# The first batch of a linear-attention and MLP kernel, rescheduled over four engines

## The chip, the cores and the metric

The kernel runs on one NeuronCore of a Trainium2 chip. The metric is the device time of one execution, in microseconds (us). TensorE (PE) does the matrix products, VectorE (DVE) and ScalarE (ACT) work on SBUF and on PSUM, [...] and SyncE (SP) issues most of the DMA transfers.

## The reference

Eight batches of eight heads, 576 positions and 64 features each go through a linear attention with cosine weights. Its output, 4608 tokens by 512, goes through an MLP with a Swish that has a factor for each hidden unit.

```python
def phi(x, c, s):
    r = np.maximum(x, 0.0)
    return np.concatenate([r * c, r * s], axis=-1)
q_p, k_p = phi(q, cos_w, sin_w), phi(k, cos_w, sin_w)   # angle pi/2 * pos / 576
kv = np.einsum('bhsf,bhsd->bhfd', k_p, v)
z = np.sum(k_p, axis=2)
num = np.einsum('bhsf,bhfd->bhsd', q_p, kv)
den = np.einsum('bhsf,bhf->bhs', q_p, z)[..., None] + 1e-06
x = (num / den)  # transposed and reshaped to 4608 x 512
h = x @ w_in     # 512 x 2048
g = h * (1.0 / (1.0 + np.exp(-beta * h)))
out = g @ w_out  # 2048 x 512
```

## The kernel before

**Tiling.** A position is p*9+n, with p from 0 to 63 on the partitions and n, the block, from 0 to 8. Two heads sit in the two halves of the partitions, and four such groups j side by side; jp counts pairs of them. A batch thus has nine blocks (n = 0 to 8) of 64 positions. The MLP takes tokens in chunks of 512, which are eight blocks: chunk 0 is blocks 0 to 7 of batch 0, and chunk 1 begins with block 8 of batch 0, followed by seven blocks of batch 1. There are nine chunks.

**One batch.** `q_relu` casts the queries to `qb` with a ReLU; PE (or, from batch 2 on, a DMA) transposes them to `qt`. `qs` is `qt` times the tangent of the angle (`tanr`), so that the cosine can be left out of numerator and denominator; `eps9` is the small constant over the cosine. `k_relu` casts the keys to `rk`. `v_scale` makes two copies of the values in `vb`, one times the cosine, one times the sine. `kv_mm` is the product of keys and values, `kv_take` its copy to SBUF. `num_mm` makes the numerators and denominators of one block for one jp (eight small matmuls), `x_rden` the reciprocal denominators, `x_mul` (DVE) or `x_mul_act` (ACT) the quotient `xs`. `x_turn_pe` transposes it on PE and copies it to `xt`, the moving operand of the MLP.

**The MLP.** Each chunk takes 32 slots. In slots 0 to 15, `h_group(c, jt)` makes one tile of 128 hidden units (four matmuls of 512 columns) and its Swish (`h_act`). In slots 16 to 31, `o_part` makes a quarter of an output tile; in chunk 0 the quarters go round, so that each block of `wout` is needed as late as can be. The weights are loaded in FP32 into four stage buffers and cast to BF16: `w_in` first, and each `w_out` block into the stage that a cast has freed. SP issues, after the first batch: w_out 0, w_out 1, value and key of batch 1, w_out 2, query of batch 1, w_out 3.

**Order.** Under `manual_schedule` each engine runs its instructions in the order in which the code issues them. The first batch is written out by hand ahead of the loop (lines 432 to 501), with dummy matmuls on zeros (`warm_pe`). Then, still ahead of the loop, the weights' casts and the first work on batch 1 are issued, in this order (lines 502 to 519):

```python
    cast_wout(0)
    cast_wout(1)
    v_scale(1, 0)
    k_relu(1)
    cast_wout(2)
    q_relu(1, 0)
```

Then the loop over the slots of chunk 0 follows. After each slot it issues what the table `early` (line 527) holds for it: block 8's transposes in slot 4, the rest of batch 1 from slot 15 on. Batches 2 to 7 are spread over the slots of the later chunks (`att_units`).

**Load gates.** Two DMAs of four bytes, `gate <- rk`, wait for key casts; on SP they stand ahead of the loads of w_in 1 and of w_in 2 and 3.

**Block 8 before.** Blocks 7 and 8 have their own PSUM banks in the first batch (4 and 6). ACT scales them, and block 8 of jp 1 comes after the xt copy.

Of the kernel before, what the change touches and what calls it, by code (L numbers as in the profile page):

```python
# [10 lines left out]
FP32 = mybir.dt.float32  # L11
BF16 = mybir.dt.bfloat16
AF = mybir.ActivationFunctionType
ALU = mybir.AluOpType
# [8 lines left out]
def kernel(  # L23
# [64 lines left out]
    def load_w(kind, i, step=4):  # L88
        if (kind, i) not in stages:
            stages[kind, i] = stage.tile([P, 4, 512], FP32, name="w_stage", tag="w_stage")  # L90
        st = stages[kind, i]
        if kind == "out":
            nc.sync.dma_start(out=st, in_=w_out_v[:, 4 * i : 4 * i + 4, :])
            return
        for a in range(0, 4, step):
            nc.sync.dma_start(out=st[:, a : a + step], in_=w_in_v[:, a : a + step, i * 512 : (i + 1) * 512])
# [41 lines left out]
    for g in range(2):  # L138
        nc.gpsimd.iota(it9[g * HP : (g + 1) * HP], pattern=[[1, NQ]], base=0, channel_multiplier=NQ,
                       allow_small_or_imprecise_dtypes=True)  # L140
    halfpi = const.tile([P, 1], FP32, name="halfpi")
    nc.vector.memset(halfpi, math.pi / 2.0)
    zero_b = const.tile([P, 1], FP32, name="zero_b")
# [8 lines left out]
    nc.scalar.activation(sin9, it9, AF.Sin, bias=zero_b, scale=ANG)  # L152
    nc.scalar.activation(warm, zero_b, AF.Silu, scale=1.0)

    zeros = const.tile([P, 512], BF16, name="zeros")
    nc.vector.memset(zeros, 0.0)
    ones = const.tile([HP, P], FP32, name="ones")
    nc.vector.memset(ones, 1.0)
    identf = const.tile([HP, HP], FP32, name="identf")
    make_identity(nc, identf)  # L160
    ident = const.tile([P, P], BF16, name="ident")
    make_identity(nc, ident)

    gate = const.tile([1, 2], BF16, name="gate")


    vb = one.tile([P, NQ, 4, 2, E], BF16, name="vb")
# [6 lines left out]

    nc.vector.reciprocal(eps9, cos9)
    nc.vector.tensor_tensor(tan9, eps9, sin9, op=ALU.mult)

    tdiag = const.tile([HP, NQ, HP], FP32, name="tdiag")
    nc.vector.tensor_tensor(
        tdiag, identf.unsqueeze(1).to_broadcast([HP, NQ, HP]),  # L180
        tan9[0:HP].unsqueeze(2).to_broadcast([HP, NQ, HP]), op=ALU.mult)
    nc.vector.tensor_scalar(eps9, eps9, scalar1=EPS, scalar2=None, op0=ALU.mult)
    for cs, t in ((0, cos9), (1, sin9)):
        nc.vector.tensor_copy(vb[:, :, :, cs, D], t.unsqueeze(2).to_broadcast([P, NQ, 4]))
# [15 lines left out]
    def q_relu(b, jp, eng="dve"):  # L200
        relu(qb[:, jp].rearrange("q n (j d) -> q j n d", j=2), raw_tile(b, "q")[:, 2 * jp : 2 * jp + 2], eng)

    def k_relu(b, j0=0, j1=4, eng="dve", n0=0, n1=NQ):
        relu(rk.rearrange("q n j d -> q j n d")[:, j0:j1, n0:n1], raw_tile(b, "k")[:, j0:j1, n0:n1], eng)

    def v_scale(b, cs, jp=None, n0=0, n1=NQ, eng="dve"):
        t = (cos9, sin9)[cs]
        rv = raw_tile(b, "v")
        js = slice(0, 4) if jp is None else slice(2 * jp, 2 * jp + 2)
        if jp is not None and eng != "act":  # L210
            if eng == "dve":
                t = ps[:, 0, 16 * cs : 16 * cs + NQ]
            (nc.gpsimd if eng == "pool" else nc.vector).tensor_tensor(  # L213
                vb[:, n0:n1, js, cs, 0:D],
                rv.rearrange("q j n d -> q n j d")[:, n0:n1, js],
                t[:, n0:n1].unsqueeze(2).unsqueeze(3).to_broadcast([P, n1 - n0, 2, D]), op=ALU.mult)
            return
        for n in range(n0, n1):
            o, a = vb[:, n, js, cs, 0:D], rv[:, js, n, :]
            if eng == "act":  # L220
                nc.scalar.activation(o, a, AF.Copy, scale=t[:, n : n + 1])
            else:
                nc.vector.tensor_scalar(o, a, scalar1=t[:, n : n + 1], scalar2=None, op0=ALU.mult)  # L223
# [6 lines left out]
    def q_turn_pe(b, jp, bank, hold=False):  # L230

        parts = ((0, 0, 5), (1, 5, NQ))
        v2 = []
        for i, n0, n1 in parts:
            t = ps[:, bank + i].bitcast(BF16)[:, 0 : (n1 - n0) * P].rearrange("q (n c) -> q n c", c=P)
            v2.append(t)
            for n in range(n0, n1):
                nc.tensor.matmul(t[:, n - n0, :], lhsT=qb[:, jp, n, :], rhs=ident,  # L238
                                 is_transpose=True, start=(n == n0), stop=(n == n1 - 1))
        def take(e, i):  # L240
            _, n0, n1 = parts[i]
            if e == "act":
                nc.scalar.copy(qt[:, jp, n0:n1], v2[i])
            else:
                tan_mul(nc.vector, qs[:, jp, n0:n1], v2[i], n0, n1)

        if hold:
            return take
        for e, i in (("act", 0), ("dve", 1), ("act", 1), ("dve", 0)):
            take(e, i)  # L250
# [22 lines left out]
    def kv_take(jps, bank, eng="dve"):  # L273
        a0, a1 = jps[0], jps[-1] + 1
        o = kv[:, :, a0:a1].rearrange("q g s c e -> q g (s c e)")
        a = ps[:, bank : bank + 2, a0 * 2 * E : a1 * 2 * E]
        if eng == "act":
            nc.scalar.copy(o, a)  # L278
        else:
            nc.vector.tensor_copy(o, a)  # L280
# [141 lines left out]
    def warm_pe(count, w=512, bank=1):  # L422
        for i in range(count):
            nc.tensor.matmul(ps[:, bank, 0:w], lhsT=zeros[:, 0:P], rhs=zeros[:, 0:w], start=True, stop=True)  # L424
# [1 line left out]
    beta = const.tile([P, JT], FP32, name="beta")  # L426
    rbeta = const.tile([P, JT], FP32, name="rbeta")

    warm_pe(78, 40)
    q_relu(0, 0, "act")  # L430
    for bank, n0, n1 in ((6, 0, 5), (7, 5, NQ)):
        nc.tensor.matmul(ps[:, bank, 0 : (n1 - n0) * HP], lhsT=ones,  # L432
                         rhs=tdiag[:, n0:n1, :], start=True, stop=True)
    for bank, n0, n1 in ((6, 0, 5), (7, 5, NQ)):
        nc.scalar.copy(tanr[:, n0:n1, :].rearrange("q n p -> q (n p)"), ps[:, bank, 0 : (n1 - n0) * HP])
    nc.tensor.transpose(ps[:, 1, 0:JT], beta16, identf[0:JT, 0:JT])
    nc.vector.tensor_copy(ps[:, 0, 0:NQ], cos9)
    nc.vector.tensor_copy(ps[:, 0, 16 : 16 + NQ], sin9)
    nc.vector.tensor_copy(beta, ps[:, 1, 0:JT])
    nc.vector.reciprocal(rbeta, beta)  # L440
    q_relu(0, 1, "dve")
    warm_pe(5, 128)
    q_turn_pe(0, 0, 4)
    warm_pe(4, 128)
    take = q_turn_pe(0, 1, 2, hold=True)
    warm_pe(9)
    take("act", 0)
    v_scale(0, 1, 0, eng="pool")
    v_scale(0, 0, 0)
    k_relu(0, 0, 2, "act")  # L450
    take("dve", 1)
    take("dve", 0)
    take("act", 1)
    kv_mm(0, 0, 6)
    v_scale(0, 1, 1, eng="pool")
    v_scale(0, 0, 1)
    kv_take((0,), 6, eng="act")
    k_relu(0, 2, 3, "act")
    k_relu(0, 3, 4, "dve", 0, 5)
    k_relu(0, 3, 4, "act", 5, NQ)  # L460

    nc.sync.dma_start(out=gate, in_=rk[0:1, 0, 0, 0:2])
    load_w("in", 1)
    nc.sync.dma_start(out=gate, in_=rk[0:1, 0, 3, 0:2])
    load_w("in", 2)
    load_w("in", 3)
    warm_pe(1, bank=1)
    for n in range(7, NQ):
        num_mm(n, 0, 4, n - 7)
    for n in range(7):  # L470
        num_mm(n, 0, 2, n)
    kv_mm(0, 1, 6)
    warm_pe(2, bank=1)
    got2 = x_rden(4, 0, 7, NQ, (0,))
    got = x_rden(2, 0, 0, 7, (0,))
    kv_take((1,), 6, eng="act")
    x_mul(got, 0, 7)
    x_mul_act(got2, 7)
    x_mul_act(got2, 8)
    for n in range(7, NQ):  # L480
        num_mm(n, 1, 6, n - 7)
    for n in range(7):
        num_mm(n, 1, 0, n)
    for gj in GJ:
        cast_win(0, gj, "pool", jps=slice(0, 1))
    for gj in GJ:
        cast_win(0, gj, "pool", 0, 256, slice(1, 2))
    x_turn_pe(0, 0, 8, 2, jps=(0,))
    got2 = x_rden(6, 0, 7, NQ, (1,))
    got = x_rden(0, 0, 0, 7, (1,))  # L490
    x_mul(got, 0, 4)
    x_mul(got, 4, 7)
    x_mul_act(got2, 7)
    h_mm(0, 0, (0, 1))
    x_turn_pe(0, 0, 4, 4, ("dve",), (1,))
    h_mm(0, 1, (0, 1))
    x_turn_pe(0, 4, 8, 5, ("act",), (1,))
    x_mul_act(got2, 8)
    h_mm(0, 2, (0, 1))
    h_mm(0, 3, (0, 1))  # L500
    for gj in GJ:
        cast_win(0, gj, "dve", 256, 512, slice(1, 2))
# [19 lines left out]
    def num_seven(jp, bank):  # L522
        for n in range(7):
# [1 line left out]

    takes = []
    early = {
        4: lambda: x_turn_pe(0, 8, 9, 7),
        15: lambda: v_scale(1, 1, eng="act"),
        22: lambda: (kv_mm(1, 0, 6), kv_mm(1, 1, 6), q_relu(1, 1), kv_take((0, 1), 6)),  # L530
        24: lambda: (cast_wout(3, "aadd"), takes.append(q_turn_pe(1, 0, 4, hold=True))),
        25: lambda: (takes.append(q_turn_pe(1, 1, 6, hold=True)),
                     [takes[jp](e, i) for jp in range(2)
                      for e, i in (("act", 0), ("dve", 1), ("act", 1), ("dve", 0))]),
        28: lambda: (num_seven(0, 4), num_seven(1, 6), x_mul(x_rden(4, 0, 0, 7, (0,)), 0, 7)),
        29: lambda: (x_turn_pe(1, 0, 7, 4, ("act",), (0,)), x_mul(x_rden(6, 0, 0, 7, (1,)), 0, 7)),
        31: lambda: ([h_mm(1, jt, (0, 1)) for jt in range(2)], x_turn_pe(1, 0, 7, 5, ("dve",), (1,)),
                     [h_mm(1, jt, (0, 1)) for jt in range(2, 4)]),
    }
# [88 lines left out]
```

## Time and profile before

| what | value |
| --- | --- |
| time, median of 3 runs | 299.46 us (298.69 to 299.69) |
| profiled execution: its own time | 301.22 us |
| profiled execution: its span | 299.4 us |
| PE busy | 286.8 us, 96% of the span |
| DVE, ACT, POOL busy | 113.8, 141.4, 74.0 us |
| mean granted PE clock | 0.989 |
| DMA over the first 60 us | 20.18 MB, mean 336 GB/s |

The span runs from the first instruction to the last; the execution's own time has 1.8 us around it. All times in the text are from the span's start. "Busy" of PE includes the drain that the profile models, so it isn't PE at its peak; the granted clock is given beside it, 1.00 for full and 0.50 for half. In a line of the timeline, the columns are start, duration, engine, line of the code, operation, out and in, shape and count, and in brackets the idle time before it and what ended that.

### The profile page before, as it was taken

The numbers are of one execution on the slowest core, as the hardware profiler recorded it, in microseconds if no ns is written. First come the engines' busy times: TensorE is split into PE (matmuls) and PEld (weight loads), VectorE is DVE, ScalarE is ACT, GpSimd is POOL, SyncE is SP. The second block draws the span as 40 slices with busy tenths as digits, with TensorE's granted clock in tenths as the row PEclk, the third lists the DMA queues.
The fourth block names the chain that finished last, engine by engine and source line by source line (L and its number), as shares of the span: only waits on it lengthen the run. The fifth ranks groups of instructions, "written<-read, shape, count | busy, mean of one in ns | idle before, by whom it ended". The sixth has DMA issues, their size and how long they took to land.

```text
span 299.4 us, 7162 instructions
## 1 busy us (share of the span) xinstructions
PE 286.8 (96%) x3042; PEld 143.7 (48%) x3068; DVE 113.8 (38%) x282; ACT 141.4 (47%) x224; POOL 74.0 (25%) x88
## 2 busy tenths in 40 slices
PE   7959999999999999999999999999999999999994
PEld 6633455445544554455445544554455444444443
DVE  3869856591860077006800680059004000000000
ACT  6645765475128512860276117611761178128511
POOL 1550000516156014701270147014701210000000
PEclk9987999999999999999999999999999999999999
DMA  7999999769699349943995299419301920131032
GB/s 244 384 341 340 390 388 391 217 138 396 123 187 376 126 63 189 345 182 66 192 315 207 48 196 342 189 39 177 86 2 20 158 48 0 37 70 35 0 72 70
DMA packets 50264, 53.82 MB, mean 180 GB/s; under 512 B 30888, under 2 KB 31160, under 8 KB 50232
## 3 DMA queue, kind: packets, MB, share of 16 engines
q1 hardware_dynamic: 47512, 46.01, 51.7%
q0 software_dynamic: 2688, 7.34, 10.5%
q8 instruction: 24, 0.39, 0.6%
q14 instruction: 8, 0.07, 0.1%
q10 hardware_dynamic: 32, 0.01, 0.0%
HBM read 36.71 MB, written 9.44 MB: 154 GB/s over the span
## 4 chain that ended last, share of the span: by engine, by line
PE 92%; DVE 3%; ACT 2%; issue 1%; DVEq 0%; ACTq 0%
PE ps L374 42%; PE ps L399 40%; PE ps L289 3%; PE ps L268 3%; PE ps L415 1%; DVE qs L226 1%; PE ps L348 1%; DVE vb L213 1%; ACT g_t L381 1%; PE ps L432 1%; PE ps L238 1%; ACT xt L353 1%; ACT L151 0%; DVE xs L311 0%; PE ps L424 0%
## 5 line engine op out<-in xcount | busy, mean ns | idle before, releaser
L374 PE MATMUL ps<-xt,win 128*128 128x512 bf16 x576 | 130.4, 384 | 2.5 <-ACT xt L353 1.1
L399 PE MATMUL ps<-wout,g_t 128*128 128x512 bf16 x536 | 120.4, 379 | 2.3 <-issue 1.5
L381 ACT ACTIVATE g_t<-ps,beta 128x512 bf16<-128x512 f32 x144 | 98.7, 688 | 37.7 <-PE ps L374 37.7
L374 PEld LDWEIGHTS <-win 128*128 128x128 bf16 x576 | 56.2, 99 | 70.4 <-issue 4.3
L399 PEld LDWEIGHTS <-g_t 128*128 128x128 bf16 x560 | 53.9, 98 | 64.3 <-issue 0.5
L394 POOL DMA_DIRECT2D out_dram<-o_sb x56 | 35.3, 634 | 148.7 <-ACT o_sb L405 148.7
L405 ACT COPY o_sb<-ps 128x512 f32<-128x512 f32 x35 | 20.5, 586 | 99.6 <-PE ps L399 99.6
L226 POOL TENSOR_TENSOR qs<-qt,tanr 128x1152 bf16<-128x1152 bf16 x12 | 29.2, 2452 | 9.1 <-DVE vb L223 8.4
L280 DVE CAST kv<-ps 128x520 bf16<-128x520 f32 x7 | 4.9, 698 | 68.1 <-PE ps L268 68.1
L418 DVE COPY o_sb<-ps 128x256 f32<-128x256 f32 x1 | 0.4, 425 | 63.2 <-PE ps L415 63.2
L311 DVE TENSOR_TENSOR xs<-ps,rden 128x768 bf16<-128x768 f32 (+3 forms) x24 | 22.3, 935 | 1.0 <-DVE rden L304 0.2
L223 DVE TENSOR_SCALAR vb<-raw_v,cos 128x256 bf16<-128x256 f32 x63 | 17.1, 346 | 0.9 <-DMA raw_v<-in_v_dram 0.9
L300 DVE TENSOR_TENSOR den<-ps,eps 128x12 f32<-128x12 f32 (+3 forms) x25 | 4.1, 162 | 33.5 <-PE ps L289 33.4
L223 DVE TENSOR_SCALAR vb<-raw_v,sin 128x256 bf16<-128x256 f32 x54 | 14.7, 346 | 0.0
L289 PEld LDWEIGHTS <-qt 64*64 64x64 bf16 x576 | 10.5, 105 | 4.2 <-issue 4.2
L289 PE MATMUL ps<-kv,qt 64*64 64x65 bf16 x576 | 11.6, 195 | 0.2 <-ACT kv L278 0.2
L289 PE MATMUL ps<-kv,qs 64*64 64x65 bf16 x576 | 11.5, 193 | 0.0
L198 DVE TENSOR_SCALAR qb<-raw_q 128x1152 bf16<-128x1152 f32 x15 | 10.6, 747 | 1.3 <-DMA raw_q<-in_q_dram 1.3
L289 PEld LDWEIGHTS <-qs 64*64 64x64 bf16 x576 | 10.5, 105 | 0.0
L268 PEld LDWEIGHTS <-rk 64*64 64x64 bf16 x576 | 8.6, 106 | 3.9 <-issue 3.3
L268 PE MATMUL ps<-vb,rk 64*64 64x130 bf16 x576 | 10.2, 218 | 0.3 <-DVE vb L213 0.2
L108 DVE CAST win<-w_stage 64x512 bf16<-64x512 f32 (+2 forms) x20 | 10.0, 502 | 0.4
(58 smaller groups left out, 101.9 us busy)
## 6 DMA issues: line engine op xcount, KB each, us to landing
raw_v<-in_v_dram SPq DMA_DIRECT2D x7, 1152.0 KB, 11.4
raw_k<-in_k_dram SPq DMA_DIRECT2D x7, 1152.0 KB, 14.3
raw_q<-in_q_dram SPq DMA_DIRECT2D x7, 1152.0 KB, 7.3
out_dram<-o_sb POOLq DMA_DIRECT2D x56, 128.0 KB, 3.6
w_stage<-in_moe_w_out_dram SPq DMA_DIRECT2D x4, 1024.0 KB, 9.8
w_stage<-in_moe_w_in_dram SPq DMA_DIRECT2D x3, 1024.0 KB, 6.6
out_dram<-o_sb SPq DMA_DIRECT2D x14, 128.0 KB, 2.4
raw_q<-in_q_dram SPq DMA_DIRECT2D x2, 576.0 KB, 3.9
```

Source lines behind the costliest of these rows:

```text
L108: nc.vector.tensor_copy(o, a)
L198: nc.vector.tensor_scalar(dst, src, scalar1=0.0, scalar2=None, op0=ALU.max)
L223: nc.vector.tensor_scalar(o, a, scalar1=t[:, n : n + 1], scalar2=None, op0=ALU.mult)
L226: eng.tensor_tensor(dst.rearrange("q n (g p) -> q n g p", g=2), src.rearrange("q n (g p) -> q n g p", g=2), tanr[:, n0:n1].unsqueeze(2).to ...
L268: nc.tensor.matmul(t[jj * HP : (jj + 1) * HP, g], lhsT=rk[hs, n, 2 * jp + jj, :], rhs=vb[hs, n, 2 * jp + jj].rearrange("q s e -> q (s e)") ...
L289: nc.tensor.matmul(ps[cols, bank + jj, slot * E : (slot + 1) * E], lhsT=(qt, qs)[cs][rows, jp, n, cols], rhs=kv[rows, g, jp, cs, :], start ...
L311: nc.vector.tensor_tensor(o.rearrange("q j n s d -> q j (n s) d"), nv[:, :, a:z, :, 0:D].rearrange("q j n s d -> q j (n s) d"), rden[:, :, ...
L374: nc.tensor.matmul(ps[:, h_bank(c, jt)], lhsT=win[jt // 4][:, mi, (jt % 4) * P : (jt % 4 + 1) * P], rhs=xt[:, :, jp, g * HP : (g + 1) * HP ...
L381: nc.scalar.activation(g_t, ps[:, h_bank(c, jt)], AF.Silu, scale=beta[:, jt : jt + 1])
L394: eng.dma_start(out=out_v[bb, n][:, m0:m1], in_=o_sb[hf * HP : (hf + 1) * HP, m0:m1])
L399: nc.tensor.matmul(o_ps, lhsT=gs[c, jt][:, tt * P : (tt + 1) * P], rhs=wout[jt // 4][:, jt % 4, :], start=(jt == 0), stop=(jt == JT - 1))
L405: nc.scalar.copy(o_sb, o_ps)
```

## The change

The first batch is written anew, and part of it is moved:

- `zeros` is set in two pieces, the first 128 columns first. The first dummies are 58 of 48 columns, not 78 of 40.
- The tangent is spread over the partitions by nine FP32 transposes with a broadcast operand, not by two FP32 matmuls on ones; `tdiag` and `ones` go. DVE copies it to SBUF, not ACT.
- Both query casts are DVE's, ahead of the copies of cosine and sine to PSUM (the second cast after them). The scaled queries take another order.
- The sine copies of the values are split: GpSimd has blocks 0 to 5 (jp 0) and 0 to 4 (jp 1), ACT the rest, one block at a time. The key cast of jp 0 is split between ACT and DVE.
- The key cast of the last group on DVE stands behind the first denominators.
- The two gates go.
- Block 8 leaves the first batch. Its numerators are issued after slot 3, its denominators and quotient after slot 4 (DVE), its transposes after slot 7.
- Block 7 of jp 1 is scaled by DVE; ACT makes both last copies to `xt`; dummies of 512 columns are put in at two more places.
- In chunk 0, batch 1's steps from slot 24 on come one slot later; the cast of w_out 3 comes two later.

```diff
-    warm_pe(78, 40)
-    q_relu(0, 0, "act")
+    warm_pe(58, 48)
     for bank, n0, n1 in ((6, 0, 5), (7, 5, NQ)):
-        nc.tensor.matmul(ps[:, bank, 0 : (n1 - n0) * HP], lhsT=ones,
-                         rhs=tdiag[:, n0:n1, :], start=True, stop=True)
+        for n in range(n0, n1):
+            nc.tensor.matmul(ps[:, bank, (n - n0) * HP : (n - n0 + 1) * HP],
+                             lhsT=tan9[0:HP, n : n + 1].to_broadcast([HP, P]), rhs=identf,
+                             is_transpose=True, start=(n == n0), stop=(n == n1 - 1))
+    nc.tensor.transpose(ps[:, 1, 0:JT], beta16, identf[0:JT, 0:JT])
     for bank, n0, n1 in ((6, 0, 5), (7, 5, NQ)):
-        nc.scalar.copy(tanr[:, n0:n1, :].rearrange("q n p -> q (n p)"), ps[:, bank, 0 : (n1 - n0) * HP])
-    nc.tensor.transpose(ps[:, 1, 0:JT], beta16, identf[0:JT, 0:JT])
+        nc.vector.tensor_copy(tanr[:, n0:n1, :].rearrange("q n p -> q (n p)"), ps[:, bank, 0 : (n1 - n0) * HP])
+    q_relu(0, 0)
+    nc.vector.tensor_copy(beta, ps[:, 1, 0:JT])
     nc.vector.tensor_copy(ps[:, 0, 0:NQ], cos9)
     nc.vector.tensor_copy(ps[:, 0, 16 : 16 + NQ], sin9)
-    nc.vector.tensor_copy(beta, ps[:, 1, 0:JT])
+    q_relu(0, 1)
+    warm_pe(8, 128, bank=0 + 2)
+    q_turn_pe(0, 0, 4)
     nc.vector.reciprocal(rbeta, beta)
-    q_relu(0, 1, "dve")
-    warm_pe(5, 128)
-    q_turn_pe(0, 0, 4)
     warm_pe(4, 128)
     take = q_turn_pe(0, 1, 2, hold=True)
-    warm_pe(9)
+    warm_pe(7)
     take("act", 0)
-    v_scale(0, 1, 0, eng="pool")
+    take("dve", 1)
+    v_scale(0, 1, 0, 0, 6, eng="pool")
+    take("act", 1)
+    v_scale(0, 1, 0, 6, NQ, eng="act")
     v_scale(0, 0, 0)
-    k_relu(0, 0, 2, "act")
-    take("dve", 1)
+    k_relu(0, 0, 2, "act", 0, 5)
+    k_relu(0, 0, 2, "dve", 5, NQ)
     take("dve", 0)
-    take("act", 1)
     kv_mm(0, 0, 6)
-    v_scale(0, 1, 1, eng="pool")
+    v_scale(0, 1, 1, 0, 5, eng="pool")
     v_scale(0, 0, 1)
     kv_take((0,), 6, eng="act")
+    v_scale(0, 1, 1, 5, NQ, eng="act")
     k_relu(0, 2, 3, "act")
-    k_relu(0, 3, 4, "dve", 0, 5)
     k_relu(0, 3, 4, "act", 5, NQ)
-
-    nc.sync.dma_start(out=gate, in_=rk[0:1, 0, 0, 0:2])
-    load_w("in", 1)
-    nc.sync.dma_start(out=gate, in_=rk[0:1, 0, 3, 0:2])
-    load_w("in", 2)
-    load_w("in", 3)
-    warm_pe(1, bank=1)
-    for n in range(7, NQ):
-        num_mm(n, 0, 4, n - 7)
+    for i in range(1, 4):
+        load_w("in", i)
+    warm_pe(1)
     for n in range(7):
         num_mm(n, 0, 2, n)
+    num_mm(7, 0, 4, 0)
+    got = x_rden(2, 0, 0, 7, (0,))
+    got2 = x_rden(4, 0, 7, 8, (0,))
+    k_relu(0, 3, 4, "dve", 0, 5)
+    warm_pe(2, bank=1)
     kv_mm(0, 1, 6)
...
     x_turn_pe(0, 0, 8, 2, jps=(0,))
-    got2 = x_rden(6, 0, 7, NQ, (1,))
     got = x_rden(0, 0, 0, 7, (1,))
+    got3 = x_rden(6, 0, 7, 8, (1,))
     x_mul(got, 0, 4)
     x_mul(got, 4, 7)
-    x_mul_act(got2, 7)
+    x_mul(got3, 7, 8)
+    warm_pe(3, bank=3)
     h_mm(0, 0, (0, 1))
-    x_turn_pe(0, 0, 4, 4, ("dve",), (1,))
     h_mm(0, 1, (0, 1))
+    x_turn_pe(0, 0, 4, 4, ("act",), (1,))
+    h_mm(0, 2, (0, 1))
     x_turn_pe(0, 4, 8, 5, ("act",), (1,))
-    x_mul_act(got2, 8)
-    h_mm(0, 2, (0, 1))
     h_mm(0, 3, (0, 1))
...
     early = {
-        4: lambda: x_turn_pe(0, 8, 9, 7),
+        3: lambda: (num_mm(8, 0, 2, 0), num_mm(8, 1, 2, 1)),
+        4: lambda: x_mul(x_rden(2, 0, 8, NQ, (0, 1)), 8, NQ),
+        7: lambda: x_turn_pe(0, 8, 9, 6),
         15: lambda: v_scale(1, 1, eng="act"),
         22: lambda: (kv_mm(1, 0, 6), kv_mm(1, 1, 6), q_relu(1, 1), kv_take((0, 1), 6)),
-        24: lambda: (cast_wout(3, "aadd"), takes.append(q_turn_pe(1, 0, 4, hold=True))),
-        25: lambda: (takes.append(q_turn_pe(1, 1, 6, hold=True)),
+        25: lambda: (takes.append(q_turn_pe(1, 0, 4, hold=True))),
+        26: lambda: (takes.append(q_turn_pe(1, 1, 6, hold=True)), cast_wout(3, "aadd"),
```

More of the change, by code (lines that the diff above doesn't have):

```diff
@@ L140 @@
                        allow_small_or_imprecise_dtypes=True)
+    zeros = const.tile([P, 512], BF16, name="zeros")
+    nc.vector.memset(zeros[:, 0:P], 0.0)
     halfpi = const.tile([P, 1], FP32, name="halfpi")
@@ L153 @@
     nc.scalar.activation(warm, zero_b, AF.Silu, scale=1.0)
[L155 to L158, printed above, removed]
+    nc.vector.memset(zeros[:, P:512], 0.0)
     identf = const.tile([HP, HP], FP32, name="identf")
@@ L162 @@
     make_identity(nc, ident)
-    gate = const.tile([1, 2], BF16, name="gate")
     vb = one.tile([P, NQ, 4, 2, E], BF16, name="vb")
@@ L176 @@
     nc.vector.tensor_tensor(tan9, eps9, sin9, op=ALU.mult)
[L178 to L181, printed above, removed]
     nc.vector.tensor_scalar(eps9, eps9, scalar1=EPS, scalar2=None, op0=ALU.mult)
@@ L463 @@
-    load_w("in", 1)
-    nc.sync.dma_start(out=gate, in_=rk[0:1, 0, 3, 0:2])
-    load_w("in", 2)
-    load_w("in", 3)
-    warm_pe(1, bank=1)
-    for n in range(7, NQ):
-        num_mm(n, 0, 4, n - 7)
+    for i in range(1, 4):
+        load_w("in", i)
+    warm_pe(1)
     for n in range(7):
         num_mm(n, 0, 2, n)
+    num_mm(7, 0, 4, 0)
[3 more added lines that the diff above has]
+    warm_pe(2, bank=1)
     kv_mm(0, 1, 6)
-    warm_pe(2, bank=1)
@@ L474 @@
-    got2 = x_rden(4, 0, 7, NQ, (0,))
-    got = x_rden(2, 0, 0, 7, (0,))
     kv_take((1,), 6, eng="act")
@@ L478 @@
     x_mul_act(got2, 7)
-    x_mul_act(got2, 8)
-    for n in range(7, NQ):
-        num_mm(n, 1, 6, n - 7)
+    warm_pe(1, bank=1)
     for n in range(7):
         num_mm(n, 1, 0, n)
+    num_mm(7, 1, 6, 0)
     for gj in GJ:
@@ L488 @@
     x_turn_pe(0, 0, 8, 2, jps=(0,))
-    got2 = x_rden(6, 0, 7, NQ, (1,))
     got = x_rden(0, 0, 0, 7, (1,))
+    got3 = x_rden(6, 0, 7, 8, (1,))
     x_mul(got, 0, 4)
     x_mul(got, 4, 7)
-    x_mul_act(got2, 7)
+    x_mul(got3, 7, 8)
+    warm_pe(3, bank=3)
     h_mm(0, 0, (0, 1))
-    x_turn_pe(0, 0, 4, 4, ("dve",), (1,))
     h_mm(0, 1, (0, 1))
+    x_turn_pe(0, 0, 4, 4, ("act",), (1,))
+    h_mm(0, 2, (0, 1))
     x_turn_pe(0, 4, 8, 5, ("act",), (1,))
-    x_mul_act(got2, 8)
-    h_mm(0, 2, (0, 1))
     h_mm(0, 3, (0, 1))
@@ L527 @@
     early = {
-        4: lambda: x_turn_pe(0, 8, 9, 7),
+        3: lambda: (num_mm(8, 0, 2, 0), num_mm(8, 1, 2, 1)),
+        4: lambda: x_mul(x_rden(2, 0, 8, NQ, (0, 1)), 8, NQ),
+        7: lambda: x_turn_pe(0, 8, 9, 6),
         15: lambda: v_scale(1, 1, eng="act"),
         22: lambda: (kv_mm(1, 0, 6), kv_mm(1, 1, 6), q_relu(1, 1), kv_take((0, 1), 6)),
-        24: lambda: (cast_wout(3, "aadd"), takes.append(q_turn_pe(1, 0, 4, hold=True))),
-        25: lambda: (takes.append(q_turn_pe(1, 1, 6, hold=True)),
+        25: lambda: (takes.append(q_turn_pe(1, 0, 4, hold=True))),
+        26: lambda: (takes.append(q_turn_pe(1, 1, 6, hold=True)), cast_wout(3, "aadd"),
                      [takes[jp](e, i) for jp in range(2)
                       for e, i in (("act", 0), ("dve", 1), ("act", 1), ("dve", 0))]),
-        28: lambda: (num_seven(0, 4), num_seven(1, 6), x_mul(x_rden(4, 0, 0, 7, (0,)), 0, 7)),
-        29: lambda: (x_turn_pe(1, 0, 7, 4, ("act",), (0,)), x_mul(x_rden(6, 0, 0, 7, (1,)), 0, 7)),
+        29: lambda: (num_seven(0, 4), num_seven(1, 6), x_mul(x_rden(4, 0, 0, 7, (0,)), 0, 7)),
+        30: lambda: (x_turn_pe(1, 0, 7, 4, ("act",), (0,)), x_mul(x_rden(6, 0, 0, 7, (1,)), 0, 7)),
         31: lambda: ([h_mm(1, jt, (0, 1)) for jt in range(2)], x_turn_pe(1, 0, 7, 5, ("dve",), (1,)),
```

## The prediction

> **What bounds the kernel now.** I read the page first: TensorE (PE) is busy 96% of the span and holds 92% of the chain of waits, so a change counts only where it moves PE. The slices then show where PE is not at full worth: the first three (22 us) are thin, and the granted clock dips there.
>
> ```profile
> PE   7959999999999999999999999999999999999994
> DVE  3869856591860077006800680059004000000000
> PEclk9987999999999999999999999999999999999999
> DMA  7999999769699349943995299419301920131032
> ```
>
> The windows put numbers on the dip: us, then busy time of PE, PEld, DVE, ACT and POOL with counts, clock, DMA share, GB/s.
>
> ```profile
> 17.00:18.20 1.20, 0.10 (x3) 0.03 (x1) 1.17 (x3) 1.10 (x2) 1.10 (x3) 1.00 0.82 172
> 18.20:19.90 1.70, 0.71 (x5) 0.30 (x5) 0.01 (x1) 0.34 (x2) 1.39 (x4) 1.00 0.85 312
> 19.90:22.40 2.50, 1.64 (x8) 0.93 (x9) 1.94 (x7) 0.83 (x3) 0.00 (x0) 0.50 1.05 405
> 22.40:26.70 4.30, 4.27 (x11) 1.48 (x11) 4.12 (x9) 1.53 (x3) 0.00 (x0) 0.50 1.02 360
> 28.30:37.80 9.50, 9.50 (x46) 4.29 (x46) 8.47 (x22) 7.67 (x12) 0.00 (x0) 1.00 1.03 387
> ```
>
> PE works 0.81 of 2.9 us from 17.0 to 19.9, then runs at half clock to 26.7 and without a hole from 28.3. DMA is full throughout. Last, the timeline of DVE and of PE, since block 8 now leaves the first batch and enters DVE's queue elsewhere:
>
> ```profile
> 31.18 3.26 DVE L117 TENSOR_SCALAR wout<-w_stage,rbeta 128x512 bf16<-128x512 f32 x8
> 35.34 2.45 DVE L223 TENSOR_SCALAR vb<-raw_v,cos 128x256 bf16<-128x256 f32 x9 [0.90 <-DMA raw_v<-in_v_dram]
> 38.36 1.36 DVE L198 TENSOR_SCALAR rk<-raw_k 128x2304 bf16<-128x2304 f32 x1 [0.57 <-DMA raw_k<-in_k_dram]
> 41.08 1.67 DVE L117 TENSOR_SCALAR wout<-w_stage,rbeta 128x512 bf16<-128x512 f32 x4 [1.36 <-DMA w_stage<-in_moe_w_out_dram]
> 44.07 1.43 DVE L198 TENSOR_SCALAR qb<-raw_q 128x1152 bf16<-128x1152 f32 x2 [1.31 <-DMA raw_q<-in_q_dram]
> 45.41 0.69 DVE L280 CAST kv<-ps 128x520 bf16<-128x520 f32 x1
> ```
>
> ```profile
> 28.21 0.27 PE L348 MATMUL ps<-ident,xs 128*128 128x128 bf16 x2
> 28.32 9.66 PE L374 MATMUL ps<-xt,win 128*128 128x512 bf16 x44
> 37.81 6.21 PE L399 MATMUL ps<-wout,g_t 128*128 128x512 bf16 x27
> ```
>
> DVE works through the second batch's operands one by one, each as it lands; the query cast waits until 44.07. Today nothing on PE needs DVE in between: block 8 is transposed at 28.21 from an xs that ACT scaled before 22.6.
>
> [...] the half-rate stretch lasts 19.89 to 26.72 us (the ends worked out of half-us means 0.89 and 0.78), 6.83 us[...]. [...] the kv cast's semaphore arrived at 45.2, it began at 45.41, when the relus ahead ended. [...] The first loads' landings, in issue order (8.8, 11.7, 13.9, 15.3 us)[...].
>
> **The change part by part.**
>
> 1. *Start, to the first value product.* 58 dummies of 48 columns at 43 ns (40 columns took 35.6) end at 3.4, as tan is ready. Nine FP32 transposes replace two FP32 matmuls (2.29 us). No row shows them; beta's alone takes 0.28; bounds 0.20 to 0.40 each; I take 0.25: 2.25. The ones memset (0.17) and tdiag (0.75) go from DVE, so PE starts them 0.85 sooner. DVE then carries what ACT did: tan copies 0.43+0.37, casts 2x0.70, small copies 0.66. Second cast ends 8.2 (7.9 before).
>
> 2. *Sin split.* GpSimd's 2.12 us becomes 1.41 and 1.18. ACT gets 7 pieces; 256 wide takes 0.50, 64 wide 0.235 (L321), so 128 wide about 0.32: 0.96+1.28. DVE: scaled queries 0.69+0.74+0.67, reciprocal 0.25, cos 1.26, four key blocks 0.5. ACT's key cast ends 12.85, so the first kv product starts about 12.9 (11.84 before). GpSimd was never last there.
>
> 3. *Second value product.* Block 8's 16 small matmuls leave, but the DVE key cast now stands behind the first denominators: first numerators 14.1 to 15.0, denominators to 15.65, cast to 16.1, kv product 16.2 (14.24 before, in earnest 14.54). Numerators end 18.4, transposes 19.0, xt copy 20.0 (18.1 before): 1.9 late.
>
> 4. *Where the head gains.* Before, third and fourth hidden tiles waited for PE transposes, ACT copy 0.59 and two ACT scalings 0.53 in bank 6, after a hole of 0.99. Now DVE scales block 7 (0.27) and three dummies (0.65) fill PE's wait. [...] the clock should stay full. Four half products 1.73, eight transposes 0.6, last copy: slot 0 at 22.65 (24.1 before), slot 4 after 8x0.216 and block 8's products 0.7 at 25.1 (27.1 before), slot 7 ends about 28.5. Carried to the end that is -2.1 us, from -2.5 to -0.8 over the bounds of step 1.
>
> 5. *No load gates.* Two tiny DMAs leave SP. The ring ran dry for about 1.1 us at 17.0 to 18.5; the w_in loads now issue as earlier ones land (to about 10.6) and stand behind the keys. w_in 2 and 3 land 1 us earlier. But w_out 0 waits for the win 0 casts, w_out 1 for win 1's, as before. DVE's casts start 20.5 (20.70 before), win 1's end 25.0 (25.4). What is queued behind w_out 1 on SP (value, key, w_out 2, query) therefore gains 0.4: the query of batch 1 lands at 43.65. Bounds: 24.5 to 26.3 for the win 1 cast give 43.1 to 44.9.
>
> 6. *Block 8 postponed: the added wait.* Its denominators and product are issued in slot 4 of the loop, that is, on DVE behind everything issued before the loop: the wout casts 0 to 2, cos, key cast and the batch-1 query cast. Its transposes stand on PE after slot 7, ahead of slot 8. PE issues matmuls in order, so it stops until DVE has come through: 43.65, cast 0.76, denominator 0.16, reciprocal 0.18, product of 256 elements 0.40 (384 took 0.55), four hops of 0.05, two transposes at half rate 0.27: slot 8 starts at **45.6**. Before, it starts 12 matmuls after 28.32: 30.9. Delay **14.7**. Steps 1 to 4 vanish in it, since PE arrives at 28.5 and waits 17 us; only step 5 counts. Behind the stalled PE stand ACT's activations of slots 8 to 15 and all of phase two; SP's loads run on.
>
> 7. *Clock after the stop.* [...] 1.7 to 3.4, I take **2.6**. (Before, 22.43 to 26.72 cost 2.1.)
>
> 8. *Slots 24 to 31 moved by one, third wout cast later.* The w_out 3 load lands by 46.8 in the trace, long before a slot 26 that now comes after 60: nothing, cover is 14 us. From slot 8 PE's work is otherwise the same and was busy 9.5 of 9.5: nothing to win back. Bounds -0.3 to +0.3.
>
> Sum: +14.7 + 2.6 = +17.3 on a span of 299.4, whose own execution took 301.22; the median of the runs, 299.46, stands 1.8 below that execution. I add to the median: **316.7 us**.
>
> **Rivals.**
> - *The block-8 product isn't held up (faster).* If it reached DVE ahead of the wout casts, the head's gain would show: 299.46-2.1 = 297.4. It needs DVE free of the query wait by 28.5, when PE arrives. Against: up to its end the ring carries 14.4 MB (batch 0 3.54, w_in 4.19, three w_out 3.15, batch 1 3.54), which at 390 GB/s are 37 us, and the code's order puts the product behind. Chance 3%. Another 1% for some canceling within 0.3%.
> - *The loads land earlier.* Without any dry ring: 1.7 us to first data, 37.0 of transfer, 2 of landing: 40.7, 2.9 earlier, 313.8. Against: SP still waits for casts, the trace's rate falls to 164 GB/s at 27 us for that reason. 5%.
> - *A longer stop.* If the head slips past its bounds[...], about 320. [...] 7%.
> - *The stop as worked out*, 84%: 43.1 to 44.9 and 1.7 to 3.4 give 315.3 to 318.8.
>
> **How the numbers follow.** The range 313.8 to 319.5 takes in the main case and the early loads. Faster is the first rival, 0.03, same 0.01, slower 0.96; 0.3% is about what a measurement of this kernel can tell.
>
> **What would show it.** In the changed profile: a hole of some 17 us on PE ahead of the block-8 transposes (L340 there), released by DVE xs; that product right after a query cast that waited for DMA; the fifth of PE's 40 slices empty and the sixth nearly so; the clock at half from about 33 to 50; slot 7 done near 28.5 with full clock from 20 to 28. Wrong if PE shows no hole before slot 8, if the query lands before 42, or if slot 8's wait ends on another engine.

## The result, and the profile after

The changed kernel takes **316.0 us** (median of 4 runs, 315.57 to 316.06), the kernel before 299.07 (298.30 to 299.69): ratio 1.056, 95% interval 1.0535 to 1.0594. Forecast were 316.7, from 313.8 to 319.5. The profiled execution of the changed kernel took 315.57, with a span of 313.8.

Some executions of the kernel before have a stretch at half clock, as the profiled one has from 20 us on (301.22, 2.15 us above the median of its runs), while the profiled execution after lies 0.4 below its own median.

The slices of the page after, tenths of busy time in 40 slices of 7.8 us:

```profile
PE   8784049999999999999999999999999999999994
DVE  5889640176549005800670085009402300000000
PEclk9999559999999999999999999999999999999999
DMA  7999996024969962995399359904900740131032
```

The fifth PE slice is empty, the fourth and sixth half so, and the clock reads 0.5 just there. DVE and DMA work on through the hole. The timeline of DVE (start, duration, engine, line, operation, shape, idle time before and its cause) shows the queue that PE waits for:

```profile
38.75 1.67 DVE L117 TENSOR_SCALAR wout<-w_stage,rbeta 128x512 bf16<-128x512 f32 x4 [1.35 <-DMA w_stage<-in_moe_w_out_dram]
41.76 0.76 DVE L190 TENSOR_SCALAR qb<-raw_q 128x1152 bf16<-128x1152 f32 x1 [1.33 <-DMA raw_q<-in_q_dram]
42.44 0.15 DVE L292 TENSOR_TENSOR den<-ps,eps 128x4 f32<-128x4 f32 x1
42.63 0.18 DVE L296 RECIPROCAL rden<-den 128x4 f32<-128x4 f32 x1
42.84 0.42 DVE L303 TENSOR_TENSOR xs<-ps,rden 128x256 bf16<-128x256 f32 x1
```

And the timeline of PE in the same stretch:

```profile
24.80 1.89 PE L366 MATMUL ps<-xt,win 128*128 128x512 bf16 x8
43.32 0.39 PE L340 MATMUL ps<-ident,xs 128*128 128x128 bf16 x2 [16.63 <-DVE xs L303]
43.51 4.75 PE L366 MATMUL ps<-xt,win 128*128 128x512 bf16 x13
```

PE ends slot 7 at 26.7 and stands 16.63 us, for two transposes that take 0.39. What they wait for is 0.42 us of DVE work whose inputs were in PSUM from 23 us on; it stands in DVE's queue behind a query cast, and that behind a transfer. The chain of waits, in order of time (start, duration, what), names the links between them (... stands for lines left out):

```profile
25.74 0.70 DVE win L108
26.45 0.02 issue
26.46 0.37 SPq L93
26.83 0.04 issue
26.87 14.87 DMA raw_q<-in_q_dram
...
41.76 0.04 DVE qb L190
...
42.84 0.43 DVE xs L303
43.27 0.05 issue
43.32 0.39 PE ps L340 x2
43.71 6.48 PE ps L366 x22
```

The last win 2 cast frees the stage buffer, SP then issues w_out 2 and behind it the query; the query takes 14.87 us from issue to landing, in which the DMA engines move 392 GB/s without a gap. That is 5.8 MB, most of it loads issued earlier (the query itself is 1.2 MB). On the chain DMA now has 8% and PE 84%, where PE had 92%.

The ring of DMA requests has no gap ahead of this either. Where the windows before, in the prediction, have 172 GB/s from 17.0 to 18.2, the changed kernel has (same columns as there, the last two are DMA share and GB/s):

```profile
17.00:18.00 1.00, 0.83 (x7) 0.32 (x5) 0.96 (x5) 0.78 (x1) 0.90 (x3) 1.00 1.05 389
18.00:19.00 1.00, 0.72 (x4) 0.36 (x4) 0.99 (x4) 0.23 (x1) 0.90 (x3) 1.00 1.08 393
```

The windows show the clock (us, busy times of PE, PEld, DVE, ACT and POOL, which is GpSimd, with counts, clock, DMA share, GB/s):

```profile
29.50:30.00 0.50, 0.00 (x0) 0.00 (x0) 0.50 (x2) 0.00 (x0) 0.00 (x0) 1.00 1.04 401
30.00:30.20 0.20, 0.00 (x0) 0.00 (x0) 0.20 (x2) 0.00 (x0) 0.00 (x0) 0.58 1.00 380
46.50:47.00 0.50, 0.50 (x3) 0.22 (x2) 0.00 (x0) 0.00 (x0) 0.00 (x0) 0.50 1.04 387
47.00:47.50 0.50, 0.50 (x4) 0.23 (x3) 0.00 (x0) 0.34 (x1) 0.00 (x0) 0.90 1.04 387
```

It drops at 30.03 (0.58 is a mean over 0.2 us, 0.03 at full) and comes back at 47.10 (0.90 over half a microsecond): 17.07 us. In the trace before, the stretch at half clock had 6.83. From 43.51 to 47.10 PE works at a clock of 0.50, and half of these 3.59 us, 1.8, is lost.

### The profile page after: what moved, and what is told of

Read it like the earlier page. It is cut to its first block, busy times and chain, and to the rows that moved or that the text cites. A ratio compares the mean times of both kernels' runs of the same rounds, so it can differ in the third digit from the quotient of the medians.

```text
span 313.8 us, 7165 instructions
## 1 busy us (share of the span) xinstructions
PE 288.5 (92%) x3058; PEld 143.6 (46%) x3058; DVE 115.2 (37%) x288; ACT 140.4 (45%) x223; POOL 74.0 (24%) x88
## 4 chain that ended last, share of the span: by engine, by line
PE 84%; DMA 8%; DVE 4%; ACT 1%; SPq 1%; issue 1%; DVEq 0%
PE ps L391 38%; PE ps L366 38%; DMA raw_q<-in_q_dram 5%; PE ps L281 3%; DMA raw_v<-in_v_dram 3%; PE ps L260 3%; DVE win L108 2%; PE ps L407 1%; DVE xs L303 1%; SPq L78 1%; PE ps L340 0%; ACT g_t L373 0%; DVE rden L296 0%; PE ps L230 0%; DVE vb L205 0%
## 5 line engine op out<-in xcount | busy, mean ns | idle before, releaser
L391 PE MATMUL ps<-wout,g_t 128*128 128x512 bf16 x560 | 124.2, 379 | 0.0
L386 POOL DMA_DIRECT2D out_dram<-o_sb x56 | 36.8, 660 | 160.1 <-ACT o_sb L397 160.1
L397 ACT COPY o_sb<-ps 128x512 f32<-128x512 f32 x35 | 20.5, 585 | 98.9 <-PE ps L391 98.9
L303 DVE TENSOR_TENSOR xs<-ps,rden 128x768 bf16<-128x768 f32 (+5 forms) x26 | 22.9, 889 | 0.9 <-DVE rden L296 0.2
L340 PE MATMUL ps<-ident,xs 128*128 128x128 bf16 x32 | 2.9, 225 | 16.9 <-DVE xs L303 16.9
L292 DVE TENSOR_TENSOR den<-ps,eps 128x12 f32<-128x12 f32 (+4 forms) x26 | 4.1, 158 | 34.9 <-PE ps L281 34.9
L190 DVE TENSOR_SCALAR qb<-raw_q 128x1152 bf16<-128x1152 f32 x16 | 11.5, 752 | 1.3 <-DMA raw_q<-in_q_dram 1.3
L345 ACT COPY xt<-ps 128x512 bf16<-128x512 bf16 (+3 forms) x5 | 3.5, 692 | 18.9 <-PE ps L340 18.8
```

What stands on the lines that cost most here:

```text
L190: nc.vector.tensor_scalar(dst, src, scalar1=0.0, scalar2=None, op0=ALU.max)
L303: nc.vector.tensor_tensor(o.rearrange("q j n s d -> q j (n s) d"), nv[:, :, a:z, :, 0:D].rearrange("q j n s d -> q j (n s) d"), rden[:, :, ...
L386: eng.dma_start(out=out_v[bb, n][:, m0:m1], in_=o_sb[hf * HP : (hf + 1) * HP, m0:m1])
L391: nc.tensor.matmul(o_ps, lhsT=gs[c, jt][:, tt * P : (tt + 1) * P], rhs=wout[jt // 4][:, jt % 4, :], start=(jt == 0), stop=(jt == JT - 1))
L397: nc.scalar.copy(o_sb, o_ps)
```

## Experiments

The theory is that of the prediction: block 8's quotient waits in DVE's queue for a transfer, and PE for it. Its rival is that something else in the new first batch holds PE back. The first four ran on one chip beside the kernel before (median 299.12); for later sets the median of the kernel before is given with them.

**Block 8 ahead in DVE's queue.** All that was issued between the win 1 casts and the loop, but for the loads of w_out 0 and 1, is issued after block 8's quotient. So more moves than block 8 alone, but the entries behind it keep their order.

```diff
+    def second():
+        (casts of win 2 and 3, the loads of v, k, w_out 2, q, w_out 3,
+         cast_wout(0) ... q_relu(1, 0), in the same order)
-        4: lambda: x_mul(x_rden(2, 0, 8, NQ, (0, 1)), 8, NQ),
+        4: lambda: (x_mul(x_rden(2, 0, 8, NQ, (0, 1)), 8, NQ), second()),
```

> The changed kernel, with block 8's denominators and quotient moved ahead of the casts of win 2 and 3 in DVE's queue; nothing else moves. Theory (the stop is DVE's queue order): PE's wait before block 8's transposes goes, slot 8 starts near 27.0 instead of 43.5 and the clock stays full, so 316.0 - 16.5 - 1.8 = 297.7, within 1 us. Rival (something else of the new first batch holds PE back: the dummies, the split, the loads without gates): PE still has a hole before slot 8 or the total stays over 305. Rival 2 (a new wait at slots 22 to 28 for the query and w_out 3 loads, now that PE is early): 299 to 301.

Measured: **297.43 us** (9 runs, 297.18 to 297.94), 0.992 of the kernel before (0.989 to 0.995). Its timeline of DVE, then of PE:

```profile
18.18 5.05 DVE L108 CAST win<-w_stage 64x256 bf16<-64x256 f32 x12
23.26 0.16 DVE L292 TENSOR_TENSOR den<-ps,eps 128x4 f32<-128x4 f32 x1
23.46 0.18 DVE L296 RECIPROCAL rden<-den 128x4 f32<-128x4 f32 x1
23.67 0.42 DVE L303 TENSOR_TENSOR xs<-ps,rden 128x256 bf16<-128x256 f32 x1
24.01 5.64 DVE L108 CAST win<-w_stage 64x1024 bf16<-64x1024 f32 x8
```

```profile
22.77 3.63 PE L366 MATMUL ps<-xt,win 128*128 128x512 bf16 x16
26.24 0.27 PE L340 MATMUL ps<-ident,xs 128*128 128x128 bf16 x2
26.35 7.38 PE L366 MATMUL ps<-xt,win 128*128 128x512 bf16 x32
```

The same three DVE instructions now end at 24.1, two microseconds before PE asks for them. There is no hole, and slot 8 starts at 26.35. Everything else of the first batch is as in the changed kernel. With the order in DVE's queue changed, all of the loss is gone, and the kernel is 1.7 us faster than the kernel before.

**The product left late, PE asks later.**

```diff
-        3: lambda: (num_mm(8, 0, 2, 0), num_mm(8, 1, 2, 1)),
-        4: lambda: x_mul(x_rden(2, 0, 8, NQ, (0, 1)), 8, NQ),
-        7: lambda: x_turn_pe(0, 8, 9, 6),
+        17: lambda: (num_mm(8, 0, 4, 0), num_mm(8, 1, 4, 1)),
+        18: lambda: x_mul(x_rden(4, 0, 8, NQ, (0, 1)), 8, NQ),
+        24: lambda: x_turn_pe(0, 8, 9, 5),
```

> The changed kernel, with DVE's order left alone, but block 8's numerators issued in slot 17, its quotient in slot 18 and its transposes in slot 24 (banks 4 and 5). Theory (only the place on PE where the product is waited for matters): PE reaches slot 24 near 42.6, the product is ready near 43.3, so a wait of under 1 us remains: 297.5 to 299. Rival (DVE's lateness costs whatever PE does, since kv's copy and the queries stand behind it): over 302.

Measured: **298.16 us** (ratio 0.995, 0.993 to 0.998). PE's timeline:

```profile
40.86 1.90 PE L391 MATMUL ps<-wout,g_t 128*128 128x512 bf16 x8
43.49 0.28 PE L340 MATMUL ps<-ident,xs 128*128 128x128 bf16 x2 [0.73 <-DVE xs L303]
```

DVE is as late as in the changed kernel (the quotient starts at 43.01). The wait is 0.73 us, because chunk 1 needs this piece only at the end of chunk 0. The lateness costs only what PE still waits for it.

**The postponement alone, in the kernel before.** The first batch stays as it was, gates included; block 8 is taken out of its numerators, denominators and scalings, and put in slots 3, 4 and 7.

```diff
-    for n in range(7, NQ):
-        num_mm(n, 0, 4, n - 7)
+    num_mm(7, 0, 4, 0)
...
-        4: lambda: x_turn_pe(0, 8, 9, 7),
+        3: lambda: (num_mm(8, 0, 2, 0), num_mm(8, 1, 2, 1)),
+        4: lambda: x_mul(x_rden(2, 0, 8, NQ, (0, 1)), 8, NQ),
+        7: lambda: x_turn_pe(0, 8, 9, 6),
```

> The kernel before, with block 8 alone postponed as in the change (numerators slot 3, quotient slot 4, transposes slot 7); the rest of the first batch as before, with gates. Theory: the postponement alone makes the loss. The query cast starts at 44.07 as before, slot 8 near 46 instead of 30.9, and 1.7 to 3.4 us go to the half clock: 315.5 to 318.5. Rival (the postponement needs the new first batch to hurt): under 305.

Measured: **316.51 us** (ratio 1.058, 1.049 to 1.066). Its PE timeline has the line

```profile
45.00 0.39 PE L348 MATMUL ps<-ident,xs 128*128 128x128 bf16 x2 [19.15 <-DVE xs L311]
```

The query cast started at 43.44 (44.07 was expected), and slot 8 at 45.18. One part of the change makes the whole loss by itself.

**PE kept busy while it waits.** `warm_pe(76, bank=7)` ahead of the transposes in slot 7 of the changed kernel.

> The changed kernel with 76 dummy matmuls of 512 columns (76 x 0.216 = 16.4 us) on PE between slot 7 and block 8's transposes, so that it isn't idle while it waits. Theory (idling costs clock beyond the wait itself): the clock stays full, slot 8 starts at the same 43.5, and the 1.8 us lost from 43.5 to 47.05 come back: 314.2, from 313.8 to 314.6. Rival (the clock after the stop costs nothing that the total shows, or the dummies run past the wait): 316.0 or more.

Measured: **313.77 us** (4 runs, 313.63 to 313.94), 2.2 us below the changed kernel's 316.0 (from its own set of runs). Two lines of its page:

```profile
PE   8689999999999999999999999999999999999994
PEclk9999999999999999999999999999999999999999
```

PE looks full and does 15.9 us of nothing (its dummies are busy 24.6 us in all, 8.7 in the changed kernel); slot 8 starts at 43.48, as before (43.51). The wait stays, its clock penalty goes: 1.8 us were expected, 2.2 came on the medians. The profiled executions differ by 1.8 us (spans 313.8 and 312.0); the other 0.4 is what the changed kernel's profiled execution lies below its median.

**The query cast alone behind block 8.** On another chip (before: 299.17).

```diff
     cast_wout(2)
-    q_relu(1, 0)
...
-        4: lambda: x_mul(x_rden(2, 0, 8, NQ, (0, 1)), 8, NQ),
+        4: lambda: (x_mul(x_rden(2, 0, 8, NQ, (0, 1)), 8, NQ), q_relu(1, 0)),
```

> The changed kernel, with batch 1's first query cast alone issued after block 8's quotient, so that block 8 stands next behind the third wout cast. Theory (the stop ends when the last transfer-bound DVE instruction ahead of block 8 does): the wout cast ends at 40.4, 2.0 us before the query cast did (42.4), so slot 8 starts near 41.5; [...] it stays half for 5.5 us and loses 2.8 instead of 1.8: 316.0 - 2.0 + 1.0 = 315.0, from 313.9 to 315.3. Rival (only the query transfer is to blame): the stop is gone, under 305.

Measured: **314.53 us** (4 runs, 313.16 to 315.15). Its PE timeline:

```profile
25.07 3.63 PE L366 MATMUL ps<-xt,win 128*128 128x512 bf16 x16
41.80 0.39 PE L340 MATMUL ps<-ident,xs 128*128 128x128 bf16 x2 [13.11 <-DVE xs L303]
```

The transposes come 1.5 us earlier, right after the third wout cast (39.34 to 41.0 on DVE). The queue has other entries bound to a transfer behind which block 8 can wait; taking one out only hands the wait to the next. The hole is shorter (13.11 us) also because slot 7 ended only at 28.7 in this execution, whose clock reads 0.7 in the slice from 15.6 to 23.5 us. After the stop half clock lasted to 46.4 (the mean clock from 46 to 47 us is 0.79), not to 47 as expected.

**Smaller parts of the change, judged from the kernel with block 8 ahead.** Three kernels first (before: 299.17), without the base kernel beside them:

```diff
-    for i in range(1, 4):
-        load_w("in", i)
+    nc.sync.dma_start(out=gate, in_=rk[0:1, 0, 0, 0:2])
+    load_w("in", 1)
+    nc.sync.dma_start(out=gate, in_=rk[0:1, 8, 3, 0:2])
+    load_w("in", 2)
+    load_w("in", 3)
```

> The kernel with block 8 ahead (median 297.43), with the two load gates put back (the second reads the last key block, block 8). Theory (the gates cost DMA time that later gaps absorb): the ring runs dry for about 1 us near 17 to 18.5, w_in 2 and 3 land 1 us later, nobody waits: 297.4 to 297.9. Rival (the missing gates are part of the gain): 298.5 or more. Rival 2 (the gates keep the key loads from sharing the ring): under 297.0.

```diff
-    warm_pe(1, bank=1)      # ahead of the numerators of jp 1
-    warm_pe(3, bank=3)      # ahead of the first hidden tile
```

> The kernel with block 8 ahead, without the four dummy matmuls of 512 columns between the second value product and the first hidden tile (one before the numerators of jp 1, three before the hidden tile). Theory A [...]: the clock drops to half at 19.9 as in the kernel before[...]: 299.1 to 300.8. Theory B [...]: 297.2 to 297.7, clock 1.00 throughout.

```diff
-    v_scale(0, 1, 0, 0, 6, eng="pool")
-    v_scale(0, 1, 0, 6, NQ, eng="act")
+    v_scale(0, 1, 0, eng="pool")
-    v_scale(0, 1, 1, 0, 5, eng="pool")
-    v_scale(0, 1, 1, 5, NQ, eng="act")
+    v_scale(0, 1, 1, eng="pool")
```

> The kernel with block 8 ahead, with the sine copies of the values all on GpSimd again (no pieces on ACT). Theory (ACT's pieces delay its key cast, which is the last to release the first value product at 11.40; GpSimd would be done at 8.6 + 2.1 = 10.7): first value product 0.6 us earlier, second unchanged since GpSimd then ends at 14.2, before the key cast at 14.7; total 296.9 to 297.4. Rival (the split is needed, as GpSimd would be the last for the second value product): 297.9 or more.

Measured: 298.41 with gates (0.997, 0.996 to 0.999), 298.37 without the late dummies (0.997, 0.995 to 0.999), 297.82 without the sine split (0.996, 0.994 to 0.998). None of the three fell into the range of a theory or of a rival. So that the base stands beside them, the first two were run again with it (before: 299.05), and one more. The last one's edit is made in the kernel before:

```diff
-    x_mul_act(got2, 7)
+    x_mul(got2, 7, NQ)
+    warm_pe(3, bank=3)
     h_mm(0, 0, (0, 1))
-    x_turn_pe(0, 0, 4, 4, ("dve",), (1,))
     h_mm(0, 1, (0, 1))
-    x_turn_pe(0, 4, 8, 5, ("act",), (1,))
-    x_mul_act(got2, 8)
+    x_turn_pe(0, 0, 4, 4, ("act",), (1,))
     h_mm(0, 2, (0, 1))
+    x_turn_pe(0, 4, 8, 5, ("act",), (1,))
     h_mm(0, 3, (0, 1))
```

> The kernel with block 8 ahead once more, so that it stands beside the next three on one chip: 297.2 to 297.9 as before (median 297.43).

> The kernel with block 8 ahead and the two load gates. In its first profile batch 1's query cast starts at 44.27 (42.47 without gates) and PE, now early, stands 0.8 us before the query transposes. Theory (the gates delay every later load, and with PE early someone waits): 0.7 to 1.3 us above the same kernel without gates. Rival (the first difference was between chips): within 0.3.

> The kernel with block 8 ahead, without the four late dummies. In its first runs three of 22 had a mean clock of 0.981 to 0.986 and 300.5 to 302.1 us, where none of nine with the dummies was below 0.992. Theory [...]: median within 0.5 us of the kernel with dummies, some executions below a clock of 0.99. Rival (no difference): none below 0.99. Rival 2 (needed always): 1 us or more in the median.

> The kernel before, with only the tail of its first batch changed: DVE scales blocks 7 and 8 of jp 1, ACT makes both last copies to xt, three dummies stand before the first hidden tile; block 8 stays in the first batch, the gates and the slots of batch 1 stay. Theory (the head's gain comes from this tail, and the gates and the slots of batch 1 then hold part of it back): slot 0 near 21 instead of 22.4 to 24.1, a wait of 1 to 2 us before the query transposes in slot 24: 298.0 to 298.9. Rival (the tail has the whole gain): 297.2 to 297.9. Rival 2 (the gain comes from the earlier steps): 299.1.

Measured: block 8 ahead 297.47, with gates 298.52, without dummies 298.12, the tail alone 299.17 (0.999, 0.997 to 1.002).

*Gates.* They cost 1.05 us, as expected. Who waits is seen in the waits of PE (engine, line, awaited: us in total, times, longest), first with gates, then without:

```profile
PE ps L261 <- ACT rk L189: 1.6, 2, 1.0
PE ps L392 <- ACT wout L115: 1.5, 2, 1.3
PE ps L392 <- issue: 1.3, 8, 0.2
```

```profile
PE ps L260 <- ACT rk L188: 1.7, 2, 1.2
PE ps L391 <- issue: 1.3, 8, 0.2
```

Of the lines shown, only the middle one has no partner. With gates the w_out 3 load lands 2.7 us later (its cast on DVE starts at 47.76, not 45.09), and output tiles in slot 28 wait 1.5 us for ACT's share of that cast. The query cast starts at 43.53, not 42.40, and PE stands 0.41 before the query transposes. This execution with gates took 300.02, 1.5 us above the median of its runs, so the waits in it are more than the usual cost. In the first profile with gates (299.13) PE waits 0.8 us for the query cast and not for w_out 3. Common to both is that loads which were hidden before come late for an early PE.

*Dummies.* Without the four late ones the median is 0.65 us higher. More than 0.5 had not been expected, and the executions under a mean clock of 0.99 that were expected did not come: the second set has none, the first three of 22, at 300.5 to 302.1 us. In 85 executions of the kernels that have these dummies and block 8 ahead there is none. That they protect the clock in some executions fits this, but was not repeated; what the 0.65 consists of stays open.

*Split.* Undoing it: PE's first value product starts at 11.25 in its profile against 11.40, the second starts at 15.64 against 14.33 and waits 0.73 us for GpSimd, so GpSimd is then last for it. But in this execution the clock reads 0.76 from 13.07 to 16.48, and the value product that starts at 11.25 takes 1.18 us (0.70 in the changed kernel): part of the 1.3 us. It was not run beside the base; that the split helps the median is not shown.

*The tail of the first batch alone* gives nothing in the total, the number of rival 2. In its profile slot 0 starts at 22.12, but the first hidden tiles wait 0.73 for GpSimd's win casts, and PE waits 0.87 for the query cast in slot 24, which still starts at 44.07, though DVE began its win casts at 18.94 instead of 20.70:

```profile
18.94 10.79 DVE L108 CAST win<-w_stage 64x256 bf16<-64x256 f32 x20
44.07 1.43 DVE L198 TENSOR_SCALAR qb<-raw_q 128x1152 bf16<-128x1152 f32 x2 [1.32 <-DMA raw_q<-in_q_dram]
```

How the gain of 1.6 us divides among the first steps, the missing gates and the later slots of batch 1 was measured for the gates only (1.05).

## Why the prediction was right, and where it was off

The prediction was right in the path: the queue, the engine that PE waits for, and the size of the wait to within 2.1 us. That its total came within 0.7 us is in part luck, as the sum below shows.

- **Step 6, the added wait: right in place and mechanism.** DVE ran query cast, denominators, reciprocal, quotient; PE's hole ends on DVE's xs. The four durations were 0.76, 0.15, 0.18 and 0.42. The two transposes took 0.39 at half clock; 0.27 is their time at full clock. Slot 8 came at 43.51 and not 45.6. Nearly all of that is the landing, the term of step 5.
- **Step 5 is the term that was mis-sized: the query landed at 41.74 and not 43.65, outside the bounds of 43.1 to 44.9.** One of the prediction's own signs of being wrong came true with it, "if the query lands before 42". Step 5 let the query follow DVE's win 1 casts, worth 0.4 us, and took nothing for it from the missing gates. But SP waits for the win 2 casts too, as the chain above shows, and the landing follows the whole ring. By the GB/s of nine profiles of this case, 14.9 to 15.5 MB have been moved when the query cast starts. The kernel before needs 44.07 us for that (the start of its query cast), at a mean of 347 GB/s, with 149 GB/s from 17.0 to 18.5 and 223 from 26.5 to 28.0; "DMA is full throughout" misread this. The changed kernel needs 41.76, at a mean of 362 GB/s, since nothing like these gaps is left. Early casts on DVE don't bring this alone: the kernel with only the tail changed, which has the gates, starts its win casts at 18.94, nearly as early as the changed kernel (18.46), and its query cast at 44.07. With block 8 ahead, the gates alone put the query cast off by 1.13 us (43.53 and 42.40). How the 2.3 us from 44.07 to 41.76 divide between the gates and the earlier casts was not measured in the changed kernel. The rival "The loads land earlier" (40.7, 5%) had the right mechanism, a ring without a gap; the landing lies between it and the main case.
- **Step 1 was too slow, and with it DVE's casts too late:** they began at 18.46 and not 20.5. The nine FP32 transposes took 1.19 us, 0.13 each, below my lower bound of 0.20; beta's single one (0.28) was no measure for nine in a row. That is 1.06 of the 1.3 us by which the query casts ended early (6.9, forecast 8.2); the rest of the 2 us came in later steps.
- **Steps 2 and 3: too late by about as much.** First value product 11.40 (12.9), second 14.76 (16.2). ACT's key cast was last for the first one, as said: it ended at 11.34.
- **Step 4: right that the clock stays full from 20 to 28; slot 7 ends at 26.7 (28.5).** From 17.0 to 19.9 PE works 2.45 of 2.9 us, against 0.81 before. That this would keep the clock was the author's estimate. But half clock was priced from the one execution in the profile. Of the executions of the kernel before on three later chips, 3 of 24, 13 of 57 and 6 of 57 had a mean clock under 0.99. They took 300.55 us or more, at medians of 299.05 to 299.17; the median execution has no such stretch.
- **Step 7, the clock: 1.8 from the trace, 2.2 by experiment, 2.6 forecast.** The forecast and its bounds of 1.7 to 3.4, which held, were the author's estimates. The half clock lay from 30.03 to 47.10, not "from about 33 to 50"; PE stopped at 26.7 (28.5) and slot 8 started at 43.51 (45.6).
- **Step 8: nothing, as said.** The w_out 3 cast starts at 60.28 without a wait for its load. Whether its two slots' delay is of use with block 8 ahead was not run.
- **The sum.** On the spans the loss is 14.4 (forecast 17.3): 12.6 for slot 8 and 1.8 for the clock, and nothing is left over. On the medians it is 16.9. The 2.9 us by which stop and clock were over-estimated were made up by a base that lay 2.15 us above its runs, and 0.4 on the other side. The prediction saw that its base execution was slow and still set the loss on the median: its span of 316.7 with the 1.8 us around it would have been 318.5 for the changed kernel. Two errors cancel, and that is luck.
- **The rival that ends faster** was refuted for this kernel, and its time, 297.4, is what the kernel with block 8 ahead takes (297.43, 297.47). That agreement is luck of the same kind: there too a head some 2 us faster than worked out met a base without the half-clock stretch.

The version with block 8 ahead beats both kernels: 0.992 (0.989 to 0.995) and 0.994 (0.992 to 0.996) of the kernel before in two sets.

## What to carry to other kernels

When a step is postponed, look at the queue of every engine that does a part of it, and ask what was issued earlier there: a small instruction inherits the wait of each transfer ahead of it, as here 0.42 us of DVE work kept PE waiting for 16.63 us. Either issue it before those, or move the place where its result is asked for; the second cost 0.7 us more here, and both took away about 18 us. When the landing of a late load is forecast, add up what the ring has to move until then and look for the gaps in it. Before a median is forecast from one profiled execution, hold its own time against the runs: what lies between the two is in that execution and not in the median.

## What the runs showed of the hardware

With 76 dummy matmuls on zeros (15.9 us) in PE's wait, the clock reads 0.9 or more in every slice, and 0.999 in the mean. With PE idle there it reads half from 30.03 to 47.10, and 0.972 in the mean.

Half clock came without a full stop too. In the kernel before, PE worked 0.81 of the 2.9 us from 17.0 to 19.9, and the clock then read half for 6.83 us. In the changed kernel it worked 2.45 us of the same stretch, and the clock read 1.00 until 30.0. How much work keeps the clock full was not measured. The time of its return differed between executions: about 46.4 with the query cast moved, 47.1 in the changed kernel.

The clock column reads 1.00 from the start, but the first microseconds are not at full rate: in the changed kernel dummies of 512 columns start 0.43 us apart from 8.23 to 9.51, and the 76 that fill the wait take 0.21 each on average (15.9 us).

Nine FP32 transposes of 64x64 with a broadcast operand took 1.19 us on PE, against 2.29 for the two FP32 matmuls that they replaced.
